# Layer 2 of batch 1 with w2 stationary, its blocks turned by VectorE, in a one-core mixing kernel

## The chip, the cores and the metric

The kernel runs on one core of a Trainium2 chip. The core has five engines that run side by side, each through its own instructions in order: TensorE (PE, matmuls; its weight loads are listed apart as PEld), VectorE (DVE), ScalarE (ACT), GpSimd (POOL) and SyncE (SP, which here only issues DMAs). POOL and ACT issue DMAs too; all DMAs share 16 DMA engines. Matmuls read SBUF and write PSUM; DVE and ACT carry PSUM results back to SBUF. The metric is the device time of one execution in microseconds (us); a lower number is better.

## The reference

Eight batches of a sequence of 3136 positions with 256 channels go through a filter in the frequency domain, then through a low-rank mix over the sequence, and then through two dense layers over the channels with a ReLU between them. The output is the sum of the mixed sequence and the dense layers' result:

```python
X = np.fft.rfft(x, axis=1)
y = np.fft.irfft(X * (filt_r + 1j * filt_i)[None], n=x.shape[1], axis=1)
xt = y.transpose(0, 2, 1)
u = y + (xt @ U @ V).transpose(0, 2, 1)
ch = np.maximum(u @ w_ch1, 0.0) @ w_ch2      # 256 -> 1024 -> 256
return (u + ch).astype(np.float32)
```

## The kernel before, in words

A position of the sequence is split as 64 q by 49 r. The transforms are matmuls: a forward one over q (`pf`, L449, written to DRAM as c1), loads of tiles `a` from c1 (`load_a`, L466), a forward one over r (`px`, L488), the product with the filter on DVE (`uv`, L507 and L509, 128 and twice 64 rows), the sum of its two halves on POOL (`y`, L512), an inverse matmul (`pi`, L524), a copy by ACT (`esb`, L528), the store as c2 (L531), and loads of tiles `e` from c2 (`load_e`, L472 to L481). From e the matmuls at L566 make the low-rank part (`h1_unit`), and `make_u` makes u of one group, transposed, with the channels on the partitions (`ut`, L609, copied by ACT at L673 or L676).

The dense layers work by groups. A full group is 4 steps (rr) of 128 positions; every batch has six, and every odd batch is followed by one small group for the last row of two batches. Batch 0 has groups 0 to 5, batch 1 groups 6 to 11 and the small group 12, batch 2 groups 13 to 18. `mm1` (L678) makes layer 1 with ReLU (`h`, eight tiles of 128 hidden channels by 512 positions). `mm2` (L693) makes layer 2 of the group before. It has two forms:

- The natural form has h stationary: for each step eight matmuls with 256 moving columns (L709), and two more with u stationary and a unit matrix moving (L713), which add the residual u. The result has positions on the partitions. DVE copies two steps at a time to `och` (`out_natural`, L722); two DMAs of 256 KB store a group (L732), issued by POOL.
- The turned form (`mm2_turned`, L744) has w2 stationary: for each step four matmuls with 512 moving columns (L754). The result has output channels on the partitions. `out_turned` (L757) adds u on DVE (L763, into `tt`), turns it in blocks of 32 by 32 on DVE (L764, into `och`), and stores a group by eight DMAs of 64 KB in runs of 256 bytes (L772), four issued by SP and four by POOL. ACT then writes `ut` in another order of positions (L673 instead of L676).

`turned` (L629) chooses the form by the constant TB: full groups of batches from TB on, except the last ones of the kernel.

The order of the work is written out by hand. The main loop (L849) goes through the groups, a from 0 to 3 in each: two tiles of `mm1`, what is due in the slot, one step of `mm2` of the group before, what is due in the next slot, then `evict` of that step (`out_natural` or `out_turned`, at odd a). So a full group is 8 slots, and a batch is SB = 48. `put` (L778) places other work into slots: `steps` (L809) has the slots of the products (L488, with the inverse matmul L524 of two products earlier): those of batch 2 stand 2.45 slots apart from slot 28 on, and those of batch 3 and later 3 slots apart, from 66 on. `load_e` is placed some slots after the last product of its tile (L819 to L828), `load_a` some slots ahead of its first (L829 to L832).

Pools set when buffers come free. px has one PSUM bank (tag x), so a product's matmul waits until DVE has read the one before. `po` has two banks (tag o), `och` two buffers, `tt` one, `uv` and `ut` three, `h` eighteen.

Of the kernel before, what the change touches and what calls it, by code (L numbers as in the profile page):

```python
# [20 lines left out]
CH = [8, 8, 9]  # L21
KG = 8
LAG = 2
TB = 2


def _consts():
# [62 lines left out]
def kernel(  # L90
# [457 lines left out]
    def one(load, *a):  # L548
        load(*a)
        yield  # L550
# [78 lines left out]
    def turned(gx):  # L629

        return groups[gx][0] >= TB and groups[gx][2] > 1 and gx + 2 < len(groups)

# [145 lines left out]
    def put(slot, gen):  # L778
        sched.setdefault(int(slot + 0.5), []).append(gen)
# [6 lines left out]
    NP = NS // 2  # L786
# [31 lines left out]
    for k, t in enumerate(steps):  # L818
        put(t, mid)  # L819
        b, m = divmod(k - LAG, NP)  # L820
        if k >= LAG and m % GP == GP - 1:
            t += 6 if b > 1 or not b and m < NP - 1 else 4
            late = SB * b + 13
            if b and t < late:
                put(max(t, SB * b - 1), one(load_e, b + 1, m // GP, (0,)))
                put(late, one(load_e, b + 1, m // GP, (1,)))
            else:
                put(t, one(load_e, b + 1, m // GP))  # L828
    for b in range(1, nb):  # L829
        for gi in range(NS // KG):  # L830
            t = steps[NP * (b - 1) + GP * gi]
# [67 lines left out]
```

## Time and profile before

| what | before |
|---|---|
| median of 3 runs | 532.53 us (531.19 to 533.56) |
| the profiled execution's own time | 529.26 us |
| its span, first to last instruction | 527.2 us |
| mean granted TensorE clock | 0.997 |
| busy: POOL, ACT | 286.7 us (54%), 378.8 us (72%) |
| L713 (residual by matmul, full groups) | 104 matmuls |
| L709 (layer 2, natural) | 448 matmuls |
| L754 (layer 2, turned) | 560 matmuls |
| L507 and L509 (products) | 96 and 192 instructions, 680 and 688 ns each |

How to read it: the span lies inside the execution's own time; the rest, 2.06 us, lies around the instructions. Busy time of PE includes the overlap of pipelined matmuls, so what a stretch of matmuls costs is read from the start of one to the start of the next. A group's line gives the source line, the engine, the operation, output <- input with shapes, the count, the busy time, the mean of one in ns, and the idle time of the engine just ahead of it with what ended it. In a timeline, the bracket at the end of a line is the idle time ahead of that line and its releaser. Line numbers are those of the kernel before; the changed kernel has the same ones.

### The profile page before, as it was taken

What the parts mean: (1) busy time and instruction counts of PE and PEld (TensorE: products, weight loads), DVE (VectorE), ACT (ScalarE), POOL (GpSimd) and SP (SyncE); (2) the same over time, 40 slices, a digit from 0 to 9 for tenths busy, and PEclk for the clock granted to TensorE, in tenths of its full rate; (3) what the DMA queues carried; (4) which work ended last, traced back from release to release, by engine and by line L of the source; (5) the groups of instructions that cost most, each with busy time, mean ns of one, the idle gap of its engine ahead of it and who ended that gap; (6) DMA issues with size and microseconds to landing.
All of it is one profiled execution on the core that took longest, in us unless ns stands there. A gap on an engine that the chain in (4) does not pass through costs nothing.

```text
span 527.2 us, 11361 instructions
## 1 busy us (share of the span) xinstructions
PE 498.6 (95%) x4022; PEld 304.1 (58%) x4022; DVE 396.0 (75%) x567; ACT 378.8 (72%) x777; POOL 286.7 (54%) x406
## 2 busy tenths in 40 slices
PE   3877899999999999999999999999999999999995
PEld 3755467767667785555555555555555555454444
DVE  6795277777877658887998888988999876446663
ACT  2685867768678768888788878887777688765551
POOL 7767453436655536685677665875666564323000
PEclk9998999999999999999999999999999999999999
DMA  8999998988988497896999798897777565644324
GB/s 135 207 201 203 194 223 187 218 218 188 228 227 222 114 212 210 190 228 159 225 221 225 184 239 214 179 249 161 186 189 153 124 165 138 136 94 81 80 67 104
DMA packets 118426, 94.58 MB, mean 179 GB/s; under 512 B 52961, under 2 KB 100770, under 8 KB 118370
## 3 DMA queue, kind: packets, MB, share of 16 engines
q0 software_dynamic: 21936, 42.52, 39.3%
q1 hardware_dynamic: 93226, 49.75, 38.1%
q10 hardware_dynamic: 3208, 1.61, 1.1%
q8 instruction: 31, 0.51, 0.4%
q14 instruction: 25, 0.20, 0.1%
HBM read 56.85 MB, written 48.17 MB: 199 GB/s over the span
## 4 chain that ended last, share of the span: by engine, by line
PE 80%; DVE 5%; DMA 4%; ACT 4%; POOL 3%; issue 2%; DVEq 0%; SPq 0%; POOLq 0%; ACTq 0%
PE phh L683 28%; PE po L754 21%; PE po L709 8%; PE px L488 5%; PE pi L524 5%; PE pu L609 4%; DVE uv L509 3%; PE pf L449 3%; DMA xt<-in_x_dram 2%; PE ph L566 2%; DVE uv L507 1%; DMA c<-asb 1%; PE po L713 1%; ACT a L378 1%; DMA ft<-in_filt_r_dram 1%
## 5 line engine op out<-in xcount | busy, mean ns | idle before, releaser
L691 ACT ACTIVATE h<-phh 128x512 f16<-128x512 f32 (+1 forms) x391 | 205.5, 578 | 71.6 <-PE phh L683 66.2
L683 PE MATMUL phh<-ut,w 128*128 128x512 f16 x768 | 197.4, 379 | 0.9 <-ACT ut L676 0.5
L512 POOL TENSOR_TENSOR y<-uv 128x512 f16<-128x512 f16 x96 | 111.1, 1158 | 110.6 <-DVE uv L509 77.6
L754 PE MATMUL po<-h,w 128*128 128x512 f16 x560 | 143.8, 379 | 0.0
L509 DVE TENSOR_TENSOR uv<-px,ft 64x512 f16<-64x512 f32 x192 | 132.1, 688 | 2.6
L683 PEld LDWEIGHTS <-w 128*128 128x128 f16 x832 | 78.5, 98 | 77.6 <-issue 2.8
L507 DVE TENSOR_TENSOR uv<-px,ft 128x512 f16<-128x512 f32 x96 | 65.3, 680 | 40.8 <-PE px L488 35.3
L772 POOL DMA_DIRECT2D out_dram<-och x120 | 70.2, 592 | 40.7 <-DVE och L764 36.9
L528 ACT CAST esb<-pi 98x512 f16<-98x512 f32 x112 | 65.8, 588 | 33.4 <-PE pi L524 30.6
L754 PEld LDWEIGHTS <-w 128*128 128x128 f16 x560 | 51.6, 98 | 53.2 <-issue 1.1
L763 DVE TENSOR_TENSOR tt<-po,ut 128x512 f32<-128x512 f32 x70 | 48.4, 692 | 32.6 <-PE po L754 30.9
L709 PE MATMUL po<-w,h 128*128 128x256 f16 x448 | 58.1, 273 | 0.0
L488 PE MATMUL px<-a,t 98*128 98x256 f16 x256 | 49.9, 277 | 6.3 <-DVE uv L509 3.3
L455 ACT CAST asb<-pf 128x512 f16<-128x512 f32 (+1 forms) x83 | 48.2, 580 | 6.2 <-PE pf L449 5.4
L764 DVE STREAM_TRANSPOSE och<-tt 128x512 f32<-128x512 f32 x70 | 49.8, 712 | 2.4
L709 PEld LDWEIGHTS <-h 128*128 128x128 f16 x448 | 42.5, 98 | 10.3 <-issue 1.1
L496 DVE TENSOR_TENSOR uv<-px,ft 128x1024 f16<-128x1024 f32 x32 | 38.1, 1220 | 10.6 <-PE px L488 10.2
L488 PEld LDWEIGHTS <-t 98*128 98x128 f16 x256 | 23.1, 99 | 32.8 <-DVE uv L509 11.2
L673 ACT CAST ut<-pu 128x512 f16<-128x512 f32 x70 | 38.2, 611 | 0.0
L524 PE MATMUL pi<-y,g 128*98 128x256 f16 x192 | 36.7, 271 | 0.5 <-POOL y L512 0.5
L449 PE MATMUL pf<-xt,w 128*128 128x512 f16 (+1 forms) x91 | 34.2, 378 | 2.7 <-DMA xt<-in_x_dram 1.6
L153 POOL DMA_DIRECT2D xt<-in_x_dram x50 | 30.3, 611 | 6.0 <-DMA xt<-in_x_dram 2.6
(92 smaller groups left out, 438.7 us busy)
## 6 DMA issues: line engine op xcount, KB each, us to landing
xt<-in_x_dram POOLq DMA_DIRECT2D x46, 256.0 KB, 6.4
a<-c SPq DMA_DIRECT2D x28, 384.0 KB
e<-c SPq DMA_DIRECT2D x56, 192.0 KB
out_dram<-och SPq DMA_DIRECT2D x160, 64.0 KB
c<-esb SPq DMA_DIRECT2D x24, 384.0 KB
c<-asb POOLq DMA_DIRECT2D x30, 256.0 KB, 4.5
out_dram<-och POOLq DMA_DIRECT2D x120, 64.0 KB, 3.2
out_dram<-och POOLq DMA_DIRECT2D x24, 256.0 KB, 4.8
```

Source lines behind the costliest of these rows:

```text
L449: nc.tensor.matmul(pf[:, 0:w], w64[:, :], xt[:, n0 * DM:n0 * DM + w], start=True, stop=True)
L488: nc.tensor.matmul(px[:, sl * DM:(sl + 1) * DM], t2[:, s * 128:(s + 1) * 128], a2[:, (2 * ml + sl) * DM:(2 * ml + sl + 1) * DM], start=Tru ...
L507: nc.vector.tensor_mul(uv[:, 0:512], px[:, :], ft[:, a:a + 512])
L509: nc.vector.tensor_mul(uv[p:p + 64, 512:1024], px[q:q + 64, :], ft[q:q + 64, b:b + 512])
L512: nc.gpsimd.tensor_add(y, uv[:, 0:512], uv[:, 512:1024])
L524: nc.tensor.matmul(pi[0:98, sl * DM:(sl + 1) * DM], g12[:, g:g + 98], y[:, o:o + DM], start=(fi == 0), stop=(fi == nf - 1), skip_group_che ...
L528: nc.scalar.copy(split(esb[:, ml * 512:(ml + 1) * 512]), natural(pi[0:98, :]))
L683: nc.tensor.matmul(pm[:, 0:w], w1[:, dh * 1024 + t * 128:dh * 1024 + (t + 1) * 128], ut[:, dh * w:(dh + 1) * w], start=(dh == 0), stop=(dh ...
L691: nc.scalar.activation(h[:, 0:w], pm[:, 0:w], RELU)
L709: nc.tensor.matmul(po[:, o:o + DM], hs[gx, t][:, rr * 128:(rr + 1) * 128], w2[:, t * DM:(t + 1) * DM], start=(t == 0), stop=False, skip_gr ...
L754: nc.tensor.matmul(po[:, :], w2[:, t * DM + dh * 128:t * DM + (dh + 1) * 128], hs[gx, t][:, :], start=(t == 0), stop=(t == 7))
L772: (nc.gpsimd if k and b < nb - 1 else nc.sync).dma_start(dst, och[32 * i:32 * i + 32, k * 512:(k + 1) * 512] .rearrange("p (r e) -> p r e" ...
```

## The change

TB becomes 1, so the six full groups of batch 1 (groups 6 to 11) take the turned form instead of the natural one: w2 stationary, the residual added by DVE, the blocks turned by DVE, and eight stores a group instead of two. Batch 0 and the small groups keep the natural form. In the placing of `load_e`, the loads for batch 2 come 6 slots after the product instead of 4; those for batch 1 and for batches from 3 on are where they were.

```diff
-TB = 2
+TB = 1
...
         b, m = divmod(k - LAG, NP)
         if k >= LAG and m % GP == GP - 1:
-            t += 6 if b > 1 or not b and m < NP - 1 else 4
+            t += 4 if not b and m == NP - 1 else 6
             late = SB * b + 13
             if b and t < late:
                 put(max(t, SB * b - 1), one(load_e, b + 1, m // GP, (0,)))
```

In the changed kernel's order of instructions SP's list has 417 rows instead of 393 and POOL's 372 instead of 360.

## The prediction

> **What bounds the kernel now.** I read the page's busy times and its chain of waits first.
>
> ```profile
> PE 498.6 (95%) x4022; PEld 304.1 (58%) x4022; DVE 396.0 (75%) x567; ACT 378.8 (72%) x777; POOL 286.7 (54%) x406
> ...
> PE 80%; DVE 5%; DMA 4%; ACT 4%; POOL 3%; issue 2%; DVEq 0%; SPq 0%; POOLq 0%; ACTq 0%
> ```
>
> TensorE (PE) is busy for 95% of the span and carries 80% of the chain. But a share is a mean over stages, so I asked for the stretch that the change touches. On PE the first layer-2 matmuls of batch 1 begin at 140.66 us and the last end at 196.2. The table of windows gives the busy time of each engine in the two parts of that stretch, and in what follows it:
>
> ```profile
> 139.00:155.00 16.00, 14.45 (x121) 10.06 (x119) 12.84 (x20) 10.90 (x22) 9.63 (x12) 1.00 0.77 205
> 155.00:198.00 43.00, 43.00 (x437) 32.31 (x436) 28.47 (x42) 32.44 (x70) 21.99 (x31) 1.00 0.78 188
> 198.00:466.00 268.00, 265.62 (x2018) 145.63 (x2016) 223.53 (x329) 213.37 (x431) 169.50 (x227) 1.00 0.78 186
> ```
>
> Columns: window, length, then PE, weight loads, DVE, ACT and POOL, the granted clock, the DMA share, GB/s. From 155 to 198 us PE has no idle time at all: what PE no longer does there comes off the span, one for one. From 139 to 155 it idles 16.00 - 14.45 = 1.55 us, so something else sets the pace there. From 198 to 466 the full groups already run in the form that batch 1 is to get: there DVE is 83% busy (223.53 of 268) and PE idles only 2.4 us. That is the best witness for the new form.
>
> **What PE saves.** The timeline of PE, one line for each run of equal matmuls (start, length, line, operands, count):
>
> ```profile
> 185.51 1.04 PE L709 MATMUL po<-w,h 128*128 128x256 f16 x8
> 186.38 0.28 PE L713 MATMUL po<-idn,ut 128*128 128x128 f16 x2
> 186.50 1.03 PE L683 MATMUL phh<-ut,w 128*128 128x512 f16 x4
> ...
> 209.24 1.03 PE L754 MATMUL po<-h,w 128*128 128x512 f16 x4
> 210.10 1.03 PE L683 MATMUL phh<-ut,w 128*128 128x512 f16 x4
> ```
>
> Lengths overlap, so cost is read from start to start. A step (one rr of a group) in the old form takes 186.50 - 185.51 = 0.99 us: 0.87 for the eight L709 and 0.12 for the two L713, which add the residual. In the new form it takes 210.10 - 209.24 = 0.86 us. The eight matmuls of 256 columns and the four of 512 thus cost nearly the same, and the saving is the residual's two. Other steps give 0.98 against 0.86; I take 0.125 us a step. Six groups of four steps are 24 steps: 24 x 0.125 = 3.0 us. The order of instructions agrees: PE's list falls from 8046 to 7758 rows, and 288 rows are 24 x 6 pairs of weight load and matmul.
>
> The Trainium skill ("TensorE: Matmul & The Clock Gate", section "Back-to-back issue gap") gives a sustained 131 ns for a matmul of 512 columns; by it the new step would take 4 x 0.131 = 0.52 us. The trace has 0.86 for the same four, 215 ns each, so the measurement decides and nothing of the sum uses the page.
>
> **What DVE, POOL and SP get.** The groups by line and shape (count | busy us, mean ns | idle before):
>
> ```profile
> L772 POOL DMA_DIRECT2D out_dram<-och x120 | 70.2, 592 | 40.7 <-DVE och L764 36.9 <-issue 3.2 <-DMA xt<-in_x_dram 0.5
> ...
> L764 DVE STREAM_TRANSPOSE och<-tt 128x512 f32<-128x512 f32 x70 | 49.8, 712 | 2.4
> L763 DVE TENSOR_TENSOR tt<-po,ut 128x512 f32<-128x512 f32 x70 | 48.4, 692 | 32.6 <-PE po L754 30.9
> ...
> L722 DVE COPY och<-po 128x512 f32<-128x512 f32 x26 | 17.9, 689 | 6.4 <-PE po L713 5.5
> ...
> L732 POOL DMA_DIRECT2D out_dram<-och x24 | 12.9, 542 | 16.4 <-DVE och L722 16.4
> ```
>
> - DVE: twelve copies L722 (689 ns) become twelve additions L763 (692) and twelve transposes L764 (712): +12 x 0.715 = 8.6 us in 59 us. Its share goes from (12.84 + 28.47) / 59 = 70% to 85%, beside 83% after 198 us.
> - POOL: twelve stores L732 become twenty-four L772: 24 x 0.592 - 12 x 0.542 = +7.7 us, from 54% to 67%. Behind them in POOL's order stand the additions y (L512, 1.15 us). PE's inverse matmuls L524 use y two steps later, some 7 us; a store group delays y by 1.3 us more than now, which that cover hides. Without cover it would cost up to 1.3 us for each of six groups.
> - SP: twenty-four stores come new (median 462 ns, 1.9 us a group), and they wait for the transposes. Behind them stand the a and e loads and the writes of c. I walked the two tightest. The a load now issued at 167.97 would move behind group 8's stores to about 175; its product starts on PE at 184.86 (now), and in the packet records this load lands within 4 us, so some 5 us remain. The e loads of batch 2 two slots later (about 3 us) sit between its writes of c, and the last, now issued at 165.04, feeds the matmuls L566 at 181.37. Cost nothing.
> - DMA engines: the same 3.1 MB leave in 12,288 packets of 256 B instead of 768 of 4 KB. By bytes of queue q1 (49.75 MB in 38.1% of 527.2 us) that is 12.7 us of all 16 engines; by packets of q1 (93,226 in the same time, 34 ns each) it is 26 us; now, by q0 (42.52 MB in 39.3%), 15 us. So between -3 and +11 us, in a stretch with 59 x 0.22 = 13 us free. I take zero, by the third window: all its full groups store so at a share of 0.78.
>
> **What hides part of the saving.** Between 139 and 155 us a product is due every 2 or 3 slots; px has one buffer, so PE's next L488 waits until DVE is done with the last product. The timelines of DVE and PE:
>
> ```profile
> 150.75 0.69 DVE L722 COPY och<-po 128x512 f32<-128x512 f32 x1
> 152.12 0.69 DVE L507 TENSOR_TENSOR uv<-px,ft 128x512 f16<-128x512 f32 x1 [0.67 <-POOL y L512]
> 152.82 1.39 DVE L509 TENSOR_TENSOR uv<-px,ft 64x512 f16<-64x512 f32 x2
> ```
> ```profile
> 154.27 0.39 PE L488 MATMUL px<-a,t 98*128 98x256 f16 x2 [1.18 <-DVE uv L509]
> ```
>
> DVE ends at 154.21, PE goes on at 154.27. Five of the 24 steps lie before this point, and their 5 x 0.125 = 0.6 us only lengthens PE's wait. I walked the chain with the new lengths (addition to next product 1.36 us, as at 207.70 to 209.06; a product 2.09; px to product 0.50; product end to PE 0.06): the addition at 144.69 pushes the product from 145.65 to 146.05, PE's next L488 from 148.13 to 148.20, and the last one from 154.27 to 154.33. So this part gains nothing and loses 0.06 us. Behind it products come every third slot, 3.5 us apart, against 2.09 + 1.36 = 3.45 us of DVE when an eviction lies between: tight, but not every interval has one. By the walk PE waits nowhere; I allow 0.1 us there and 0.1 us where batch 1 ends (197 us).
>
> **The sum.** 19 steps x 0.125 = 2.4 us, less 0.06, 0.1 and 0.1: 2.1 us. The span goes from 527.2 to 525.1. The profiled execution took 529.26, that is 2.06 around the span, so it would take 527.2. The median of the runs, 532.53, stands 3.3 above that execution; with the same distance the time is 530.4 us, -0.4%.
>
> **Rivals.**
> 1. *The whole saving.* The 1.55 us of waiting comes from phases that may fall otherwise. If none of it hides a step, all 3.0 us come off; if the early part then idles at the third window's rate (2.4 / 268 x 16 = 0.14 us), another 1.4. 529.5 down to 528.1. Against it: the walk finds the same chain of products. 0.20.
> 2. *Waits take it all.* With DVE at 85%, rows L488 <-DVE grow: 0.17 us at each of the 12 evictions is 2.1 us. About 532.5. For it: the interval of 3.45 against 3.5. Against it: the third window, with 2.4 us of idle time in all. 0.17.
> 3. *Slower: och's two buffers.* The first L764 of a group waits until the stores of the group two before have landed, four of which now go through SP, in order behind e loads that wait for writes of c (the waits of SP show one of 8.3 us). From one group's last transpose (152.2) to the next but one's first (164.5) there are 12.3 us, less 1.9 of issue and 3.2 to 7.3 until landing (as POOL's L772): slack of 3.1 to 7.2 us. If SP holds stores 8.3 us, DVE stands still 1.1 to 5.2, say 3.2 us, and PE behind it; for two groups 6.4, net +4.3: 536.8. It decides from a hold of 3.1 us on. Against it: the two slots more let c land before SP reaches the load. 0.08.
> 4. *Slower: the packets.* If the +11 us of DMA time count, and a third falls where the share is full (0.95 to 0.97 in windows 155 to 165 and 185 to 198), 3.7 us come on the path, net +1.6: 534.1. The Trainium skill ("DMA: Bandwidth & Descriptors", section "Specifications") speaks for this: below 512 B a transfer misses line rate, by a read-modify-write. The third window speaks against it. 0.03.
>
> That the change does not do what it says is excluded by the order of instructions.
>
> **The numbers.** The forecast's case has 0.52 and by itself spans 529.3 to 531.6 (the walk's doubt of 0.6 us each way and the runs' scatter). The range of 528.1 to 533.0 takes in rivals 1 and 2 and leaves out 3 and 4. A measurement of this kernel tells about 0.5%, 2.7 us, from no change. Faster by more: rival 1 nearly whole (0.17) and the forecast's better end (0.13), 0.30. Slower by more: rival 3 and part of 4, 0.10. Between: 0.60.
>
> **What would show it.** In the profile after: L713 down by 48, L754 up by 96, L764 up by 12; from 155 to the end of batch 1 PE without idle time and 2.4 us shorter; still a wait of L488 on DVE near 154 us, now of some 1.6 us; DVE near 85%. It is wrong if PE shows new waits on DVE (L488), POOL (L524) or a DMA (a, e) in batch 1, or if L764 waits for stores.

## The result, and the profile after

The changed kernel takes 530.2 us (median), beside 533.56 for the kernel before in the same set of runs: ratio 0.9921 with a 95% interval of 0.9894 to 0.9948. Two later sets of the same kernel, on other occasions, gave 0.9946 (0.9917 to 0.9976) and 0.9949 (0.9918 to 0.9980). So the gain is 0.5 to 0.8%, 2.7 to 4.2 us; the forecast was 530.4 us and -0.4% of 532.53. The ratios compare the fast executions of both kernels alone, and two of the changed kernel's 17 in the first set, of 536.17 and 1305.83 us, count as slow and are left out.

The span of the one profile shown is 528.4 us, longer than the 527.2 before. The busy times and the shares of the chain, from the page of the changed kernel:

```profile
PE 494.1 (94%) x3878; PEld 291.0 (55%) x3878; DVE 403.6 (76%) x579; ACT 379.0 (72%) x777; POOL 295.0 (56%) x418
...
PE 78%; DMA 9%; DVE 6%; POOL 2%; ACT 1%; issue 1%; SPq 1%; ACTq 0%; DVEq 0%; POOLq 0%
```

PE has 144 matmuls less and 4.5 us less of busy time; DMA's share of the chain went from 4 to 9%. That is the start of the kernel, where both kernels do the same work in the same order: there this execution waited longer for loads, and the first low-rank matmuls of batch 1 (L566) end at 122.55 us instead of 118.79. In the profiles of this study that point lies anywhere from 118.8 to 127.6 us, and the mean granted clock between 20 and 60 us anywhere from 0.76 to 0.96. One span against another therefore says nothing about 3 us. I compare from that point on.

The windows of the changed kernel, moved so that each holds the same work as the three rows shown in the prediction (columns as there):

```profile
142.76:158.76 16.00, 13.99 (x91) 7.37 (x89) 14.03 (x22) 10.94 (x22) 10.43 (x14) 1.00 0.79 191
158.76:199.46 40.70, 40.70 (x323) 22.76 (x322) 34.87 (x52) 32.41 (x70) 27.14 (x37) 1.00 0.80 186
199.46:466.00 266.54, 264.45 (x2014) 145.21 (x2012) 223.51 (x329) 212.80 (x430) 170.63 (x228) 1.00 0.79 189
```

PE's matmuls are 30 fewer in the first part and 114 fewer in the second, which is 5 and 19 steps of six. The first part is as long as before, 16.00 us, though PE does less in it: its idle time grew from 1.55 to 2.01 us. The second part went from 43.00 to 40.70 us and is still without idle time on PE. That is the whole effect on these two parts: -2.30 us, and none of it in the first five steps. DVE is now 86% busy in both parts together (48.90 of 56.70 us).

The timeline of PE in the changed kernel shows both halves:

```profile
155.19 0.38 PE L488 MATMUL px<-a,t 98*128 98x256 f16 x2
155.41 0.38 PE L524 MATMUL pi<-y,g 128*98 128x256 f16 x2
155.63 1.02 PE L683 MATMUL phh<-ut,w 128*128 128x512 f16 x4
158.04 0.39 PE L488 MATMUL px<-a,t 98*128 98x256 f16 x2 [1.38 <-DVE uv L509]
...
163.29 1.03 PE L754 MATMUL po<-h,w 128*128 128x512 f16 x4
164.15 1.03 PE L683 MATMUL phh<-ut,w 128*128 128x512 f16 x4
```

A step costs 164.15 - 163.29 = 0.86 us, as read ahead. The wait at L488 is there and has grown from 1.18 to 1.38 us. Counted from the first L488 that waits for DVE in these windows it ends at the same moment: 158.04 - 143.11 = 14.93 us, against 154.27 - 139.35 = 14.92 in the kernel before.

The groups of the changed kernel that answer to those of before:

```profile
L772 POOL DMA_DIRECT2D out_dram<-och x144 | 84.2, 591 | 48.1 <-DVE och L764 40.5
...
L763 DVE TENSOR_TENSOR tt<-po,ut 128x512 f32<-128x512 f32 x82 | 56.7, 692 | 34.5 <-PE po L754 32.5
L764 DVE STREAM_TRANSPOSE och<-tt 128x512 f32<-128x512 f32 x82 | 58.4, 712 | 3.2 <-DMA out_dram<-och 0.4
```

Counts and lengths are as forecast (twelve more of each on DVE, twenty-four more on POOL). One thing is new: L764 has an idle time ended by the landing of a store, 0.4 us. It comes back below.

### The profile page after: what moved, and what is told of

It is laid out like the page before. It is cut to its first block, busy times and chain, and to the rows that moved or that the text cites. A ratio compares the mean times of both kernels' runs of the same rounds, so it can differ in the third digit from the quotient of the medians.

```text
span 528.4 us, 11158 instructions
## 1 busy us (share of the span) xinstructions
PE 494.1 (94%) x3878; PEld 291.0 (55%) x3878; DVE 403.6 (76%) x579; ACT 379.0 (72%) x777; POOL 295.0 (56%) x418
## 4 chain that ended last, share of the span: by engine, by line
PE 78%; DMA 9%; DVE 6%; POOL 2%; ACT 1%; issue 1%; SPq 1%; ACTq 0%; DVEq 0%; POOLq 0%
PE phh L683 28%; PE po L754 26%; PE px L488 5%; PE pi L524 5%; DMA xt<-in_x_dram 4%; PE po L709 4%; PE pu L609 4%; DVE uv L509 3%; PE pf L449 3%; PE ph L566 2%; DVE uv L507 1%; DMA e<-c 1%; DMA g<-gd 1%; DMA a<-c 1%; DMA c<-asb 1%
## 5 line engine op out<-in xcount | busy, mean ns | idle before, releaser
L683 PE MATMUL phh<-ut,w 128*128 128x512 f16 x768 | 197.4, 379 | 0.9 <-ACT ut L676 0.5
L754 PE MATMUL po<-h,w 128*128 128x512 f16 x656 | 168.5, 379 | 0.0
L683 PEld LDWEIGHTS <-w 128*128 128x128 f16 x832 | 79.1, 98 | 81.3 <-issue 2.8
L772 POOL DMA_DIRECT2D out_dram<-och x144 | 84.2, 591 | 48.1 <-DVE och L764 40.5
L754 PEld LDWEIGHTS <-w 128*128 128x128 f16 x656 | 60.3, 98 | 61.7 <-issue 1.3
L763 DVE TENSOR_TENSOR tt<-po,ut 128x512 f32<-128x512 f32 x82 | 56.7, 692 | 34.5 <-PE po L754 32.5
L764 DVE STREAM_TRANSPOSE och<-tt 128x512 f32<-128x512 f32 x82 | 58.4, 712 | 3.2 <-DMA out_dram<-och 0.4
L488 PE MATMUL px<-a,t 98*128 98x256 f16 x256 | 50.0, 277 | 9.4 <-DVE uv L509 3.9
L673 ACT CAST ut<-pu 128x512 f16<-128x512 f32 x82 | 44.7, 612 | 0.0
L488 PEld LDWEIGHTS <-t 98*128 98x128 f16 x256 | 23.1, 99 | 38.1 <-DVE uv L509 12.7
L449 PE MATMUL pf<-xt,w 128*128 128x512 f16 (+1 forms) x91 | 34.0, 376 | 4.8 <-DMA xt<-in_x_dram 3.6
L524 PE MATMUL pi<-y,g 128*98 128x256 f16 x192 | 36.7, 272 | 0.0
L709 PE MATMUL po<-w,h 128*128 128x256 f16 x256 | 33.2, 273 | 0.0
L609 PEld LDWEIGHTS <-e 96*128 96x128 f16 x686 | 26.4, 98 | 9.0 <-issue 0.4
```

Of the source, the lines that this page charges most:

```text
L488: nc.tensor.matmul(px[:, sl * DM:(sl + 1) * DM], t2[:, s * 128:(s + 1) * 128], a2[:, (2 * ml + sl) * DM:(2 * ml + sl + 1) * DM], start=Tru ...
L524: nc.tensor.matmul(pi[0:98, sl * DM:(sl + 1) * DM], g12[:, g:g + 98], y[:, o:o + DM], start=(fi == 0), stop=(fi == nf - 1), skip_group_che ...
L683: nc.tensor.matmul(pm[:, 0:w], w1[:, dh * 1024 + t * 128:dh * 1024 + (t + 1) * 128], ut[:, dh * w:(dh + 1) * w], start=(dh == 0), stop=(dh ...
L754: nc.tensor.matmul(po[:, :], w2[:, t * DM + dh * 128:t * DM + (dh + 1) * 128], hs[gx, t][:, :], start=(t == 0), stop=(t == 7))
L763: nc.vector.tensor_add(tt, po[:, :], uts[gx][:, dh * 512:(dh + 1) * 512])
L764: nc.vector.transpose(och.rearrange("p (j h a) -> p h j a", h=2, a=32)[:, dh], tt.rearrange("p (j t) -> p j t", t=32))
```

## The experiments

For every run I give the ratio to the kernel before, and the length of one stretch of its profile, from the end of L566 of batch 1 to the start of L566 of batch 3. It holds all of batch 1's layer 2 and leaves the scattered start out. In the kernels with the natural form it is 122.4 us in both profiles with the old spacing. Its two ends in the kernel before (241.22 less 118.79, the end of the first row):

```profile
117.00 1.79 PE L566 MATMUL ph<-e,ul 64*32 64x256 f16 x49
241.22 1.59 PE L566 MATMUL ph<-e,ul 64*32 64x256 f16 x49
```

And in the first profile of the changed kernel (242.46 less 122.55):

```profile
121.29 1.26 PE L566 MATMUL ph<-e,ul 64*32 64x256 f16 x37 [0.39 <-DMA e<-c]
242.46 1.59 PE L566 MATMUL ph<-e,ul 64*32 64x256 f16 x49
```

| run | ratio (95%) | stretch, us |
|---|---|---|
| before | | 122.43 |
| the change, first set | 0.9921 (0.9894 to 0.9948) | 119.91 |
| again | 0.9946 (0.9917 to 0.9976) | 120.65 |
| again2 | 0.9949 (0.9918 to 0.9980) | 120.64 |
| tb_only | 0.9935 (0.9905 to 0.9964) | 120.85 |
| shift_only | 1.0003 (0.9974 to 1.0031) | 122.41 |
| res_pe | 0.9981 (0.9941 to 1.0021) | 121.82 |
| twice_turn | 1.0065 (1.0030 to 1.0099) | 125.47 |
| px2 | 1.0066 (1.0038 to 1.0094) | 119.74 |
| sp_stores | 0.9932 (0.9895 to 0.9970) | 121.04 |
| tb0 | 1.0016 (0.9982 to 1.0049) | 121.09 |
| respace | 0.9926 (0.9893 to 0.9958) | 120.08 |
| respace_nat | 0.9996 (0.9967 to 1.0024) | 122.70 |

**again and again2: the change by itself, twice more.** No edit.

> The changed kernel unaltered, timed beside the kernel before and the next three on one chip. Theory (PE sets the pace; 19 of 24 steps lose 0.125 us, the other five are hidden by the wait of px on VectorE): 2.1 to 2.5 us less than before, ratio 0.9953 to 0.9960; from the end of the low-rank matmuls of batch 1 (L566) to the start of those of batch 3 some 2.4 us less than in the profile of before. Rival (something outside the batch-1 stretch gains as well, as the first ratio of 0.9921 suggests): 3.5 to 5 us less.

> The changed kernel once more beside the kernel before, since two ratios of it differ (0.9921 and 0.9946). Theory: 2.1 to 2.9 us less, ratio 0.9945 to 0.996. Rival (there is a gain outside the stretch): 3.5 to 5 us less, ratio 0.991 to 0.9935.

Measured: 2.9 and 2.7 us less by the ratios (0.0054 of 535.07 and 0.0051 of 534.32), and 1.8 us less in the stretch. Both gains lie over the 2.1 to 2.5 us that were expected of again, the second within the 2.1 to 2.9 expected of again2, and the 1.8 of the stretch lies under the expected 2.4. The rival's 3.5 us and more stands only in the first set (4.2 us by its ratio), and as again's interval is 1.3 to 4.4 us, the times alone don't decide between the two. The stretch is 0.74 us longer than in the first profile, and all of it lies at one place, the end of batch 1. DVE in the run again:

```profile
194.62 0.69 DVE L763 TENSOR_TENSOR tt<-po,ut 128x512 f32<-128x512 f32 x1 [0.56 <-PE po L754]
197.21 0.71 DVE L764 STREAM_TRANSPOSE och<-tt 128x512 f32<-128x512 f32 x1 [1.90 <-DMA a<-c]
198.02 0.69 DVE L763 TENSOR_TENSOR tt<-po,ut 128x512 f32<-128x512 f32 x1
```

POOL in the same run:

```profile
188.46 2.34 POOL L772 DMA_DIRECT2D out_dram<-och  x4 [2.98 <-issue]
```

And PE in the same run:

```profile
201.50 0.39 PE L488 MATMUL px<-a,t 98*128 98x256 f16 x2 [1.01 <-DVE uv L509]
```

The transpose at 197.21 is the first of group 11. By the order of instructions it waits for the eight stores of group 9, whose buffer it takes over; the profile puts the wait down to the DMA that landed last, a load. POOL's four of these stores began only at 188.46, after 2.98 us of idle time for which the profile has no cause. The last of the four, issued at 190.22, lands at 196.93, and the transpose follows 0.28 us later. DVE then stands still for 1.90 us, and PE's L488 at 201.50 for 1.01 us. The first profile has the same 2.98 us of idle time on POOL, but there the last store, issued at 190.84, lands sooner, at 196.10: the same L764 waited 0.45 us and L488 0.25. This is the third rival's mechanism (two buffers of och), at one group instead of two, through POOL and not through SP, and at a price of some 0.75 us (1.01 less 0.25).

**tb_only and shift_only: one half of the change each.**

```diff
# tb_only, against the changed kernel
-            t += 4 if not b and m == NP - 1 else 6
+            t += 6 if b > 1 or not b and m < NP - 1 else 4
```

> Only the form of layer 2 is changed; the e loads of batch 2 stay 4 slots after the product. Theory (the two slots cost and bring nothing by themselves): the same time as the changed kernel within 0.5 us, or 2.1 to 2.5 us less than before. Rival (the stores on SP need the e loads out of their way): waits of L764 on stores, or of L488 and L566 on a and e loads, appear in batch 1, and the time is 2 to 6 us longer than that of the changed kernel.

```diff
# shift_only, against the kernel before
-            t += 6 if b > 1 or not b and m < NP - 1 else 4
+            t += 4 if not b and m == NP - 1 else 6
```

> Only the e loads of batch 2 are moved two slots later; layer 2 of batch 1 keeps the natural form. Theory: no change against before within 0.5 us. Rival (the move itself is worth time, so that it explains the part of the first ratio that the theory does not): 1.5 to 3 us less than before.

tb_only gives 0.9935, 3.5 us less than before, and a stretch of 120.85 us, some 0.2 us over again and again2; its waits are nearly those of again (L764 2.10 us beside 1.90, L488 1.22 beside 1.01). shift_only gives 1.0003 and a stretch of 122.41 us, that of before. Both rivals fall: within what the runs can tell (0.3%) the later e loads cost nothing, bring nothing, and are not needed here.

**res_pe: the residual back on PE, in the turned form.**

```diff
-                             hs[gx, t][:, :], start=(t == 0), stop=(t == 7))
+                             hs[gx, t][:, :], start=(t == 0), stop=(t == 7 and b > 1))
+        if b == 1 and a % 2:
+            nc.tensor.matmul(po[:, :], idn[:, :], uts[gx][:, dh * 512:(dh + 1) * 512],
+                             start=False, stop=True)
...
-        nc.vector.tensor_add(tt, po[:, :], uts[gx][:, dh * 512:(dh + 1) * 512])
+        if b == 1:
+            tt = po
+        else:
+            ...
+            nc.vector.tensor_add(tt, po[:, :], uts[gx][:, dh * 512:(dh + 1) * 512])
```

> The changed kernel with the residual of batch 1 added by PE again: one matmul of 512 columns with the unit matrix stationary per half group (L713's work in the turned form, 12 x 0.215 us = 2.6 us), and the transpose reads PSUM, so the addition L763 goes. PE's list is then 24 x 0.86 + 2.6 = 23.2 us against 23.8 natural, VectorE's is as before, stores and e loads are as in the changed kernel. Theory (the gain is what PE no longer does): 0.3 to 0.8 us less than before, so 1.5 to 2 us more than the changed kernel. Rival (the gain lies in the stores, the form or the e loads): as fast as the changed kernel within 0.5 us.

Ratio 0.9981, -1.0 us with an interval of -3.2 to +1.1; stretch 121.82 us, 0.61 less than before, inside the expected 0.3 to 0.8, and 1.2 to 1.9 more than in the profiles of the changed kernel. The run puts the residual back on PE and keeps form, stores and e loads; VectorE loses the addition L763 and so has less to do than in the changed kernel, and yet most of the stretch's gain is gone. So most of the gain in the stretch is the residual's matmuls. A small part is not: in the kernel before and in shift_only one L524 inside the stretch waits for POOL's y (0.24 and 0.23 us), and neither res_pe nor the changed kernel has that wait.

**twice_turn: every transpose of batch 1 twice.**

```diff
+        if b == 1:
+            nc.vector.transpose(och.rearrange("p (j h a) -> p h j a", h=2, a=32)[:, dh],
+                                tt.rearrange("p (j t) -> p j t", t=32))
         if a == 3:
```

> The changed kernel with every transpose of batch 1 done twice (12 more of 0.71 us, same result). Theory (VectorE has cover from 159 us on only as long as an interval of products holds 2.09 + 1.36 us; with 2.07 us it is 4.16 against 3.25 to 3.7 us): PE waits at L488 for nearly every eviction, 0.4 to 0.7 us each, 5 to 8 us more than the changed kernel. Rival (VectorE is far from setting the pace): under 2 us more.

Ratio 1.0065, so 3.5 us over before and 6 to 8 over the changed kernel; the stretch is 125.47 us, 4.8 to 5.6 more. PE's waits in this run:

```profile
152.98 0.39 PE L488 MATMUL px<-a,t 98*128 98x256 f16 x2 [0.86 <-DVE uv L509]
159.83 0.39 PE L488 MATMUL px<-a,t 98*128 98x256 f16 x2 [2.13 <-DVE uv L509]
170.87 0.39 PE L488 MATMUL px<-a,t 98*128 98x256 f16 x2 [0.66 <-DVE uv L509]
...
207.22 0.39 PE L488 MATMUL px<-a,t 98*128 98x256 f16 x2 [2.19 <-DVE uv L509]
```

The size is as expected, the spread is not: not nearly every eviction costs 0.4 to 0.7 us, but single ones cost 0.3 to 2.2 us and others nothing, because the next interval without an eviction gives DVE time back. Twelve times 0.71 us, 8.5 us of DVE, cost 5 us: one more such instruction at each eviction, and VectorE sets the pace of the stretch.

**px2: two banks for px, three for tag m.** Tag m holds the results of L683, L609 and L449 among others.

```diff
-    BUFS = {"x": 1, "f": 1, "m": 4, "o": 2}
+    BUFS = {"x": 2, "f": 1, "m": 3, "o": 2}
```

> The changed kernel with two PSUM banks for px and three instead of four for tag m; every engine's order stays the same. Theory (the five hidden steps are hidden by px's single bank): the waits of L488 on VectorE near 143 to 158 us (0.19 + 0.31 + 1.38) and near 201 and 207 us go, PE saves up to 1.9 + 0.6 us more, if three banks carry tag m: then 1.5 to 2.5 us less than the changed kernel. Rival (tag m needs its fourth bank): new waits of L683, L609 and L449 on ScalarE, and 3 to 15 us more than the changed kernel.

Theory and rival hold, each in its place. Between 140 and 215 us PE has no wait at L488 any more, so the single bank was the cause of those waits; from the end of L566 of batch 1 to the start of that of batch 2 the kernel takes 60.25 us instead of 61.25. That is 1.00 us, of 1.88 us of waits that are gone. But elsewhere the kernel is slower, with the same order of instructions: from L566 of batch 3 to that of batch 7 it takes 225.64 us instead of 221.97, and the whole is 0.66% slower than before. There px has its second bank too, so tag m's fourth bank is the one thing that is missing; that it is the cause is argued from this, since the profile lists only four waits of 0.23 to 0.25 us on ScalarE there, while PE's busy time for as many matmuls rises from 220.45 to 223.05 us.

**sp_stores: all stores of batch 1 on SP.**

```diff
-                (nc.gpsimd if k and b < nb - 1 else nc.sync).dma_start(
+                (nc.gpsimd if k and 1 < b < nb - 1 else nc.sync).dma_start(
```

> The changed kernel with all eight stores of a group of batch 1 issued by SP, none by POOL. Theory (the wait of group 11's transpose comes from POOL's late stores of group 9): that wait goes, and with it 0.1 to 0.9 us at L488 near 201 us; 0 to 0.9 us less than the changed kernel. Rival (SP's order is what is tight: 1.9 us more a group ahead of a and e loads): waits of L488 or L566 on loads, or of L764 on stores of SP, 1 to 4 us more.

Ratio 0.9932 (0.9895 to 0.9970), not to be told from the changed kernel's. The profiled execution took 536.19 us beside a median of 530.1, but the 61.24 us behind L566 of batch 1 are as in the other profiles. In it group 11's first L764 has no wait and the L488 near 205 us waits 0.25 us, so the wait that POOL's late stores caused is gone, as expected; but the products of batch 4 now meet a late a load (1.0 us at L488), which is the rival, small. The two cancel, and the stretch is 121.04 us.

**tb0: the turned form for batch 0 too.**

```diff
-TB = 1
+TB = 0
```

> The turned form for batch 0 as well (TB = 0). If the saving of 0.125 us a step held there, another 3.0 us would go. Theory (it holds only where no product chain binds; in batch 0's layer 2 products are due every 1.3 slots, some 2 us, VectorE's share in 60 to 139 us would go from 71 to 82%, and the DMA engines are at 0.92 to 0.95): the chain of px binds at most evictions, and the time is 0 to 5 us more than the changed kernel. Rival (PE's saving counts in full): 2 to 3 us less than the changed kernel.

Ratio 1.0016, so the further 3.0 us do not come, and some 4 us are lost against the changed kernel. The profile (this run's fastest execution, 531.04 us beside a median of 534.87) shows one large wait of PE:

```profile
119.59 2.93 PE L566 MATMUL ph<-e,ul 64*32 64x256 f16 x49 [4.15 <-DMA a<-c]
```

L566 needs the last e loads of batch 1, and in SP's order eight stores of batch 0 now stand among the loads between 95 and 118 us. The px chain that the theory named shows only in small waits up to 110 us (0.23, 0.45 and 0.24 us). Behind L566 it shows more: the waits of L488 on DVE between 122 and 185 us sum to 3.03 us instead of 1.88, and from L566 of batch 1 to that of batch 2 the kernel takes 62.44 us instead of 61.25. So in this execution one part of the loss lies with loads at the start and 1.2 us with DVE; what the slower executions lose more was not seen.

**respace and respace_nat: other slots for the products.**

```diff
-    steps = [7.6 + 1.3 * k for k in range(NP)] + [28 + 2.45 * k for k in range(NP)]
+    steps = [7.6 + 1.3 * k for k in range(NP)] + [28, 30, 33, 35, 38, 40, 42, 45, 47, 50, 52, 55, 58, 61, 64, 67]
...
-        steps += [SB * (b - 2) + 18 + 3 * k for k in range(NP)]
+        steps += [SB * (b - 2) + (22 + 2.8 * k if b == 3 else 18 + 3 * k) for k in range(NP)]
```

> The changed kernel with the products of batches 2 and 3 placed otherwise: none is less than 3 slots after the one before from slot 55 on until 73 (they stood at 57, 60, 62, 65, 66), then 2.8 slots apart. Theory (the five hidden steps are hidden by px at these short intervals): the waits of L488 on VectorE of 0.31 and 1.38 us near 146 and 158 us go, and nothing takes their place; 1.2 to 1.9 us less than the changed kernel from the end of L566 of batch 1 to its start for batch 2. Rival (the wait moves to another interval): waits of L488 of the same sum elsewhere, same time as the changed kernel within 0.5 us.

> The kernel before (natural form in batch 1) with the products placed as in the run respace. Theory: its wait of 1.18 us near 154 us goes too, so it gains 1.0 to 1.5 us on the kernel before, and stays 24 x 0.125 = 3.0 us behind respace, since no step is hidden any more. Rival (the two forms differ by the 2.1 to 2.5 us whatever the spacing): 2.1 to 2.5 us behind respace.

respace: ratio 0.9926, like the changed kernel. The wait of 1.38 us near 158 us is gone, and up to L566 of batch 2 the kernel is 2.3 us quicker (58.93 us), but some products have moved past that point; up to L566 of batch 3 it is 120.08 us, as in the changed kernel. The waits came back later, where the shorter intervals of batch 3 stand:

```profile
202.96 0.39 PE L488 MATMUL px<-a,t 98*128 98x256 f16 x2 [0.71 <-DVE uv L509]
205.61 0.39 PE L488 MATMUL px<-a,t 98*128 98x256 f16 x2 [0.31 <-DVE uv L509]
208.26 0.39 PE L488 MATMUL px<-a,t 98*128 98x256 f16 x2 [0.32 <-DVE uv L509]
...
218.10 0.39 PE L488 MATMUL px<-a,t 98*128 98x256 f16 x2 [0.52 <-DVE uv L509]
```

With 0.19 and 0.25 us further ahead the waits of L488 on DVE in the stretch sum to 2.30 us, beside 0.19 + 0.31 + 1.38 + 0.25 + 0.31 = 2.44 us in the first profile of the changed kernel: the rival, the wait only moved. With the natural form this placing does not show the 1.0 to 1.5 us that were expected either (0.9996; 122.70 us). Between the two forms lie 2.62 us of stretch here, more than in again (1.8) and less than the full 3.0; by the ratios they are 3.7 us apart, which does not tell theory from rival.

## Why the prediction was right, point by point

- **PE's saving of 0.125 us a step**: right. 24 steps, 0.86 to 0.88 us each but for one that runs into a wait of L488, and res_pe takes most of it back by putting the residual's matmuls back.
- **Five steps hidden by the product chain**: right. Walked: 0.06 us lost up to the end of the wait; measured 0.01. The wait grew to 1.38 us (walked: about 1.6). px2 shows that px's one bank makes this wait.
- **19 steps in full**: right, 2.30 us measured in the second part against 2.4, with no wait of PE in it.
- **POOL's longer store groups at nothing**: right. No L524 of the changed kernel waits for y behind the start.
- **Later e loads at nothing**: right (shift_only, tb_only).
- **256-byte packets at nothing**: right in size, but the 12,288 packets did not come. In the packet records only SP's queue q1 has more packets of 256 B, 6,144 of them; POOL's queue q0 has 384 of 4 KB less, so POOL's stores still stand there as packets of 4 KB, though their runs in DRAM are 256 B long. By the two pages q0 and q1 together took 77.4% of 527.2 us, 408.1 us, before and 77.1% of 528.4, 407.4 us, after; the range was -3 to +11. The Trainium skill's 512-byte rule ("DMA: Bandwidth & Descriptors", section "Specifications"), the ground of the fourth rival, shows no effect on these times.
- **0.1 us at the end of batch 1**: mis-sized. There the first L764 of group 11 waits for stores, and L488 waits 0.25 to 1.22 us in four profiles of the turned form. The third rival had the right buffers and the wrong queue. By the prediction's own list this counts against it: L764 waiting for stores, and a new wait of L488 on DVE, were named there as signs of being wrong.
- **The size of the whole**: -0.4% forecast, -0.5 to -0.8% measured. The 530.4 us beside 530.2 are luck to 1 us: the sum starts from a median of 532.53 us, and in the set of the result the kernel before took 533.56. The sum lacked a term outside the stretch. POOL has idle times without a recorded cause ahead of some DMA issues, always at the same places of one kernel's list. In the kernels with the natural form one of 1.57 to 1.59 us falls at 333 to 340 us, in a stretch where POOL has no slack, and y then comes late for PE. The timeline of POOL in the kernel before:

```profile
333.46 1.73 POOL L772 DMA_DIRECT2D out_dram<-och  x3 [1.59 <-issue]
```

  PE in the kernel before:

```profile
344.70 0.38 PE L524 MATMUL pi<-y,g 128*98 128x256 f16 x2 [0.24 <-POOL y L512]
```

  PE in the run respace_nat:

```profile
349.79 0.38 PE L524 MATMUL pi<-y,g 128*98 128x256 f16 x2 [1.89 <-POOL y L512]
```

  shift_only has the same wait with 0.51 us. In the profiles of the changed kernel the idle times stand elsewhere (2.98 us near 189, 2.09 us near 407) and this wait of L524 does not occur. So 0.2 to 1.9 us more come off there, by where POOL's idle times fall. From the end of L566 of batch 1 to the end of the kernel the natural form takes 408.4 (before), 409.6 (shift_only) and 410.3 us (respace_nat), the changed kernel 405.9, 406.7 and 406.5 and tb_only 406.8: 1.6 to 2.6 us less than before and 2.7 to 3.7 less than shift_only, beside 2.7 to 4.2 by the three ratios. So the lower ratios are covered and the 4.2 is not, but its interval begins at 2.8. In shift_only 0.70 us of this is a wait of L488 for a late load of a near 292 us, so it is not all POOL's. That POOL's idle times make up what the timed runs gain beside the stretch is argued from profiles and was not tried by itself.

  Where POOL pauses follows a count. Each DMA's operands in the trace list the pieces that it writes: 256 for one L772, 64 for one L732. Summed over POOL's DMAs up to the pause, these are 13,096 and 40,680 in the changed kernel, 26,664 and 40,808 in the kernel before, 13,032 and 41,064 in sp_stores, 26,984 and 54,120 in tb0, all within some 520 of a multiple of 13,550. POOL's part of a group counts 1,024 pieces in the turned form and 128 in the natural one, and so the change moved the pauses. At two multiples that are missing here POOL is idle as well, with a releaser in the profile (2.15 us at 26,792 in the changed kernel, 2.07 us at 12,904 in the kernel before). What is used up at that count stays open.

## What to carry to other kernels

Here the part in which PE had no idle time gave a saving on PE nearly in full, and the part in which it waited gave none of it: cut the window at the waits before multiplying a saving by a count. The wait that came from a rate (one product per so much VectorE time) moved when the schedule was moved and went only with another buffer, whose bank had to come from somewhere. Compare two profiles from a point behind the scattered start, not by their spans.

## What was not expected of the hardware

- Executions of the same instruction order differ by up to 7 us at the end of L566 of batch 1: it lies at 118.8 to 125.9 us in the eleven profiles other than px2 and tb0, with a mean granted clock of 0.76 to 0.96 between 20 and 60 us. Behind that point, the first stretch of 61.2 us is the same within 0.02 us in the three profiles of the changed kernel and in tb_only (61.25, 61.24, 61.25, 61.23).
- POOL stands idle 1.0 to 3.7 us ahead of some DMA issues without a releaser in the profile: in all three profiles of the changed kernel after 111 and after 246 of POOL's 287 DMAs, in other kernels elsewhere, and near each further 13,550 pieces that its DMAs have written.
- POOL's stores of 64 KB in runs of 256 B stand in the packet records as packets of 4 KB, those of SP as packets of 256 B.
